# Opening of a layernorm, FFT and Mish kernel: rows centred on ScalarE, roots taken by pairs, w1 scaled in four parts

## The chip, the cores and the metric

One core of a Trainium2 chip runs the whole program. The metric is device time in us, the median of several executions. The engines are TensorE (PE, with its weight loads PEld), VectorE (DVE), ScalarE (ACT), GpSimd (POOL) and SyncE (SP, which here only issues DMAs). Each runs its own list of instructions in order and waits on semaphores of the others.

## The reference

x is 2048 rows of 512; w1 is 512 x 1792, w2 is 1792 x 512. All of it is float32.

```python
xn = (x - mean(x)) / sqrt(var(x) + 1e-5)               # by row
A  = irfft2(rfft2(xn) * (w_r + 1j * w_i), s=(2048, 512))
h  = einsum("bsd,df->bsf", xn, w1) + b1
B  = einsum("bsf,fd->bsd", h * tanh(softplus(h)), w2)  # Mish between
return x + A + B
```

## The kernel before

**Numbers.** A float32 operand is split into two float16 parts, a high half (scaled and rounded, on ScalarE) and a low half (the rest, on VectorE), and a product is three matmuls: high by high, high by low, low by high. The scales are powers of two, got from a norm of the data.

**Work.** The 2048 rows are taken in 4 groups `g` of 4 tiles `s` of 128 rows. Normalized rows `xh` feed two branches. In the MLP branch, `up(n)` makes one tile `ph` of 128 hidden units by 512 rows (12 matmuls of 512 columns, from `w1t` and the transposed rows `xnT`), `mish(n)` is ScalarE's function from `ph` to `hb`, `a_hi(n)` and `a_lo(n)` split the result, and `down(n)` adds it into `pa` with w2 (12 matmuls). There are 56 `up` and 56 `down`. In the spectral branch, `s1_mm` is the first stage of the transform along the rows (bank psS, emptied by `s1_out`, stored by `s1_store`), and later stages are `p2_unit`, `spectrum` (banks `dre`, `dim`; result split into `u`), `dp_unit` (bank psA, emptied into `at`, sent by DMA into `ai`), `ip_unit` (psT, `tt`) and `s1_inverse` (psY).

**Order.** `opening()` and `middle()` are written out by hand, and each engine does their steps in the written order. From there a scheduler interleaves the streams by priority. PSUM banks come from three pools: `ps_f` (2), `ps_h` (2), `ps_a` (4); a new tile waits until the old one in its bank is emptied. `big` has 5 SBUF buffers for the chunks of w1, then of w2.

**The opening.** `warm` makes 24 matmuls on a tile of zeros, which no result uses. x's first group comes in two DMAs of 512 KB, then part of the constants and w1 in 7 chunks. VectorE computes mean and variance of four tiles (`stats`, `aggr`); `root_by_table` takes the root of all four variances (ScalarE's Sqrt), loads ScalarE's table for Mish, and makes `rs` (the inverse deviation times 1024) and `nb` (minus mean times `rs`). By tile, ScalarE's `hi` makes the high half from x, `rs` and `nb`; VectorE's `full` makes the float32 row `xs` and `lo` subtracts the high half. TensorE turns the halves (`turn_to`, 4 matmuls with the identity, into `pt`), and `place_from` copies them into `xnT`. w1's chunks are scaled in three parts (chunk 0, chunk 1, chunks 2 to 6): `norm_w1` takes the squares' sum on ScalarE (or a bound from the maximum on VectorE), `sum_w1` is GpSimd's sum over the partitions, `scale_w1` makes the scale `ip_w`, `w1_hi` and `w1_lo` split, `exp_w1` makes the scale that `mish` undoes. `act_scale` makes the scale `ip_a` of `a` from all parts. `up_pair(0)` and `up_pair(2)` make the first four `ph`, all high by high first; `up(4)` and on go one by one.

Functions that the diff touches, and their callers, with the line numbers of the profile:

Of the kernel before, what the change touches and what calls it, by code (L numbers as in the profile page):

```python
# [19 lines left out]
P = 128  # L20
# [16 lines left out]
def spectral_mlp_kernel(ctx, tc, x, wt, w0, w1, b1, w2, cT, cIT, cM, out):  # L37
# [71 lines left out]
    class Rows:  # L109

        def __init__(self, g, x4):
# [6 lines left out]
            self.xh, self.xs, self.pt = {}, {}, {}  # L118
# [7 lines left out]
        def root_by_table(self):  # L126
            var = self.mv[:, :, 1]
            eps = sp.tile([P, 1], F32, tag="eps", name="eps")
            nc.gpsimd.memset(eps, 1e-5)
            d, v, y, t, z, k = (  # L130
                sp.tile([P, 4], F32, tag=f"{tag}4", name=f"{tag}_0", bufs=2)
                for tag in ("rd", "rv", "ry", "rt", "rz", "rk")
            )
# [126 lines left out]
    def norm_w1(k, engine):  # L260
        part = min(k, 2)
# [27 lines left out]
    def w1_hi(k):  # L289
        fs = slice(2 * k * P, 2 * (k + 1) * P)  # L290
        nc.scalar.activation(w1t[:, 0, :, fs], w1st[k], AF.Copy, scale=sc["w1", min(k, 2)])

    def w1_lo(k):
# [4 lines left out]
            sc["w1", min(k, 2)],  # L298
# [562 lines left out]
    def opening():  # L861
# [16 lines left out]
        for s in range(4):  # L878
            r.stats(s)
            if s:  # L880
                r.aggr(s - 1)
# [452 lines left out]
```

## Time and profile before

| | |
|---|---|
| median of 3 runs | 373.16 us (372.67 to 373.53) |
| profiled execution, its own time | 373.16 us |
| its span, from the first to the last instruction | 371.4 us |
| TensorE busy | 364.4 us (98%) |
| VectorE busy | 250.0 us (67%) |
| ScalarE busy | 170.6 us (46%) |
| granted TensorE clock | 1.000 |

The execution's time is 1.76 us more than its span. Times in rows count from the span's start. Busy time of TensorE includes the 24 products on zeros, and its matmuls are pipelined: a record lasts longer than the distance to the next one.

### The profile page before, as it was taken

How to read it: one execution, taken by the hardware profiler on the slowest of the kernel's cores; microseconds unless marked ns; L12 is line 12 of the kernel's file. 1: busy time of each engine (PE TensorE's matmuls, PEld its weight loads, DVE VectorE, ACT ScalarE, POOL GpSimd, SP SyncE). 2: the span in 40 equal slices, each digit the busy share in tenths (PEclk: the TensorE clock that was granted, in tenths of full speed). 3: DMA queues.
4: the chain of work that ended last, by engine and by line, in shares of the span. 5: the costliest groups of instructions: out<-in, count | busy, mean ns of one | idle time of the engine just before them, and what ended most of it. 6: DMA issues, size and time to landing. Idle time of an engine off the chain costs nothing.

```text
span 371.4 us, 5651 instructions
## 1 busy us (share of the span) xinstructions
PE 364.4 (98%) x2093; PEld 186.0 (50%) x2093; DVE 250.0 (67%) x471; ACT 170.6 (46%) x257; POOL 46.7 (13%) x48
## 2 busy tenths in 40 slices
PE   8899999999999999999999999999999999999996
PEld 3544444544544455444555455544545444445564
DVE  4878998654467754599888866878479854424354
ACT  3889986424533533433544353445435444523100
POOL 0110003302203300203030303030030300000000
PEclk9999999999999999999999999999999999999999
DMA  8844921697673588036302360105931234549535
GB/s 280 262 135 158 327 62 28 175 336 235 192 181 124 103 220 277 8 115 238 102 3 71 103 187 39 43 23 164 282 115 46 65 90 98 128 93 339 222 142 199
DMA packets 56012, 55.79 MB, mean 150 GB/s; under 512 B 16128, under 2 KB 44704, under 8 KB 55216
## 3 DMA queue, kind: packets, MB, share of 16 engines
q1 hardware_dynamic: 55984, 55.43, 48.7%
q8 instruction: 16, 0.26, 0.3%
q14 instruction: 12, 0.10, 0.1%
HBM read 35.46 MB, written 12.58 MB: 129 GB/s over the span
## 4 chain that ended last, share of the span: by engine, by line
PE 90%; DVE 3%; DMA 3%; ACT 1%; SPq 1%; issue 1%; ACTq 0%; DVEq 0%
PE ph L642 38%; PE pa L65 12%; PE pa L64 12%; PE pa L61 12%; PE psP L454 1%; PE psY L61 1%; DMA x<-in_x_dram 1%; PE psY L65 1%; PE psP L464 1%; PE psY L64 1%; PE psT L61 1%; PE psS L64 1%; PE psS L61 1%; PE psT L65 1%; PE psS L65 1%; PE psT L64 1%
## 5 line engine op out<-in xcount | busy, mean ns | idle before, releaser
L642 PE MATMUL ph<-xnT,w1t 128*128 128x512 f16 x672 | 153.7, 379 | 0.0
L642 PEld LDWEIGHTS <-w1t 128*128 128x128 f16 x672 | 65.1, 98 | 74.0 <-issue 0.2
L653 ACT ACTIVATE hb<-ph,b1t,fp_exp 128x512 f32<-128x512 f32 x56 | 43.2, 773 | 77.4 <-PE ph L642 77.3
L65 PE MATMUL pa<-w2t,a 128*128 128x512 f16 x181 | 68.6, 379 | 0.0
L61 PE MATMUL pa<-w2t,a 128*128 128x512 f16 x181 | 68.6, 379 | 0.0
L64 PE MATMUL pa<-w2t,a 128*128 128x512 f16 x181 | 68.6, 379 | 0.0
L665 DVE SCALAR_TENSOR_TENSOR a<-hb,ip_a,a 128x512 f16<-128x512 f32 x46 | 35.9, 783 | 37.4 <-ACT a L662 37.2
L662 ACT ACTIVATE a<-hb,ip_a 128x512 f16<-128x512 f32 x46 | 32.9, 719 | 1.0
L65 PEld LDWEIGHTS <-a 128*128 128x128 f16 x190 | 18.6, 98 | 21.0
L61 PEld LDWEIGHTS <-a 128*128 128x128 f16 x190 | 18.6, 98 | 19.2
L64 PEld LDWEIGHTS <-a 128*128 128x128 f16 x190 | 18.6, 98 | 18.9
L194 POOL TENSOR_TENSOR xh<-xs,xh 128x512 f16<-128x512 f32 x12 | 15.7, 1308 | 62.8 <-ACT xh L178 32.9
L610 DVE SCALAR_TENSOR_TENSOR tt<-psT,tt 128x512 f16<-128x512 f32 x16 | 11.0, 686 | 17.3 <-ACT tt L609 17.3
L469 DVE SCALAR_TENSOR_TENSOR z<-psP,z 128x512 f16<-128x512 f32 x16 | 10.9, 690 | 13.6 <-ACT z L468 13.6
L178 ACT ACTIVATE xh<-x,nb,rs 128x512 f16<-128x512 f32 x16 | 12.7, 803 | 13.0 <-DVE nb L169 12.9
L363 ACT ACTIVATE u<-w,sc_u 128x512 f16<-128x512 f32 x16 | 10.8, 713 | 15.4 <-DVE w L563 7.0
L609 ACT ACTIVATE tt<-psT 128x512 f16<-128x512 f32 x16 | 9.5, 592 | 17.6 <-PE psT L65 13.9
L586 ACT ACTIVATE at<-psA 128x512 f16<-128x512 f32 x16 | 9.4, 586 | 13.3 <-PE psA L65 10.3
L468 ACT ACTIVATE z<-psP 128x512 f16<-128x512 f32 x16 | 9.5, 594 | 12.3 <-PE psP L464 12.3
L364 DVE SCALAR_TENSOR_TENSOR u<-w,sc_u,u 128x512 f16<-128x512 f32 x16 | 11.5, 748 | 5.4 <-ACT u L363 5.4
L97 ACT ACTIVATE y<-psS 128x512 f16<-128x512 f32 x16 | 9.3, 589 | 12.0 <-PE psS L65 12.0
L98 DVE SCALAR_TENSOR_TENSOR y<-psS,y 128x512 f16<-128x512 f32 x16 | 10.9, 686 | 5.8 <-ACT y L97 5.8
(204 smaller groups left out, 566.4 us busy)
## 6 DMA issues: line engine op xcount, KB each, us to landing
wm<-in_wt_dram SPq DMA_DIRECT2D x8, 512.0 KB
ai<-at SPq DMA_DIRECT2D x64, 64.0 KB
d_t<-tt SPq DMA_DIRECT2D x32, 128.0 KB
w1s<-in_w_dram SPq DMA_DIRECT2D x7, 512.0 KB
w2s<-in_w_dram SPq DMA_DIRECT2D x7, 512.0 KB
d_y<-y SPq DMA_DIRECT2D x7, 512.0 KB
m<-in_x_dram SPq DMA_DIRECT2D x3, 1024.0 KB
yt<-d_y SPq DMA_DIRECT2D x6, 512.0 KB
```

The costliest lines, as they stand in the source:

```text
L61: first = nc.tensor.matmul(ps, stat(0), mov(0), start=start, stop=False)
L64: nc.tensor.matmul(ps, stat(0), mov(1), start=False, stop=False)
L65: nc.tensor.matmul(ps, stat(1), mov(0), start=False, stop=stop)
L98: nc.vector.scalar_tensor_tensor(y1v[:, :, 1, :], psv, 2.0**-17, y1v[:, :, 0, :], op0=ALU.mult, op1=ALU.subtract)
L178: nc.scalar.activation(xh[:, 0, :], self.x[s], AF.Identity, scale=self.rs[:, s : s + 1], bias=self.nb[:, s : s + 1])
L194: engine.tensor_sub(self.xh[s][:, 1, :], self.xs[s], self.xh[s][:, 0, :])
L364: nc.vector.scalar_tensor_tensor(dst_l, src, scale, dst_h, op0=ALU.mult, op1=ALU.subtract)
L610: nc.vector.scalar_tensor_tensor(tt[:, :, 1, :], ps, 2.0**-12, tt[:, :, 0, :], op0=ALU.mult, op1=ALU.subtract)
L642: nc.tensor.matmul(ph[n + k], w1t[:, hw, dc, f * P : (f + 1) * P], xnT[g][:, hx, dc, :], start=(hw, hx, dc) == (0, 0, 0), stop=(hw, hx, dc ...
L653: nc.scalar.activation(hbt[n], ph.pop(n), AF.Mish, bias=b1t[:, f : f + 1], scale=s_exp[part_of(f)])
L662: nc.scalar.activation(act[n][:, 0, :], hbt[n], AF.Copy, scale=sc["a"])
L665: nc.vector.scalar_tensor_tensor(act[n][:, 1, :], hbt.pop(n), sc["a"], act[n][:, 0, :], op0=ALU.mult, op1=ALU.subtract)
```

## The change

Row 0 of x has a DMA of its own. Each tile is centred on ScalarE as soon as its mean is there (`xc` = mean minus x), and the roots are taken for two tiles at a time. The sign goes into `nk` (minus 1024 by the approximate inverse root) and `rs`, which one Newton step refines from it. The high half is `xc` by `nk`, on ScalarE. The low half is `xc` by `rs` less the high half, one VectorE instruction instead of two. The high half no longer waits for the Newton step. The table for Mish is loaded later, after w1's second square. Warming is 13 products, and 3 more stand between the first turns. Two tiles are placed by one copy. w1's chunks 2 to 6 become two parts (2 and 3; 4 to 6), and the first chunk's high half is made in two pieces. `s1_out` of tiles 0 and 1 goes from the opening into `middle`. In `dp_unit`, the two instructions that empty psA have high priority.

```diff
-        def root_by_table(self):
-            var = self.mv[:, :, 1]
...
-            nc.scalar.activation(d, var, AF.Sqrt, bias=eps)
-            nc.scalar.preload_act_table_set("mish")
-            nc.vector.tensor_scalar(v, var, 1e-5, -0.5, op0=ALU.add, op1=ALU.mult)
...
+        def root_by_table(self, lo, hi):
...
+            nc.scalar.activation(d, var, AF.Sqrt, bias=self.eps)
+            yield
             nc.vector.reciprocal(y, d)
...
+            nc.vector.tensor_scalar(k, y, -1024.0, None, op0=ALU.mult)
+            yield
+            nc.vector.scalar_tensor_tensor(t, y, -0.5, y, op0=ALU.mult, op1=ALU.mult)
+            nc.vector.scalar_tensor_tensor(z, var, 1e-5, t, op0=ALU.add, op1=ALU.mult)
+            nc.vector.scalar_tensor_tensor(rs, z, 1.5, k, op0=ALU.add, op1=ALU.mult)
+            yield
+
+        def centre(self, s):
+            nc.scalar.activation(self.xc[s], self.x[s], AF.Identity, scale=-1.0, bias=self.mv[:, s, 0:1])
+
+        def hi_centred(self, s):
+            self.xh[s] = tp.tile([P, 2, D], F16, tag=f"w{s}", name=f"xh_{s}")
+            nc.scalar.activation(self.xh[s][:, 0, :], self.xc[s], AF.Copy, scale=self.nk[:, s : s + 1])
+
+        def lo_centred(self, s):
+            xh = self.xh[s]
+            nc.vector.scalar_tensor_tensor(
+                xh[:, 1, :], self.xc[s], self.rs[:, s : s + 1], xh[:, 0, :], op0=ALU.mult, op1=ALU.subtract
+            )
...
-    W1_PARTS = [(0, 1), (1, 2), (2, 7)]
+    W1_PARTS = [(0, 1), (1, 2), (2, 4), (4, 7)]
...
+            with tc.high_priority():
+                nc.scalar.mul(at[:, :, 0, :], ps, 2.0**-15)
+                nc.vector.scalar_tensor_tensor(
+                    at[:, :, 1, :], ps, 2.0**-15, at[:, :, 0, :], op0=ALU.mult, op1=ALU.subtract
+                )
...
-        warm(24)
+        idle = warm()
+        idle(13)
         x0 = tp.tile([P, 4, D], F32, tag="z", name="x_0")
-        for a in (0, 2):
-            nc.sync.dma_start(x0[:, a : a + 2, :], xv[:, a : a + 2, :])
+        for a, b in ((0, 1), (1, 2), (2, 4)):
+            nc.sync.dma_start(x0[:, a:b, :], xv[:, a:b, :])
...
+        turn(0, 0)
+        turn(1, 0)
+        idle(3)
+        place(0, 0, DVE)
+        r.lo_centred(3)
+        scale_w1(0)
...
+        place(0, 1, ACT)
+        place(1, 0, DVE)
+        w1_hi(0, 0, 1)
+        w1_hi(0, 1, 2)
+        place(1, 1, DVE)
         norm_w1(1, ACT)
         sum_w1(1)
-        norm_w1(2, ACT)
+        nc.scalar.preload_act_table_set("mish")
         w1_lo(0)
         scale_w1(1)
         exp_w1(0)
         w1_hi(1)
-        norm_w1(3, ACT)
+        norm_w1(3, DVE)
+        norm_w1(2, ACT)
+        sum_w1(2)
         up_pair(0, (0, 1), (1, 0))
+        mish(0)
+        w1_lo(1)
         norm_w1(5, DVE)
         norm_w1(4, ACT)
-        norm_w1(6, DVE)
-        sum_w1(2)
-        mish(0)
-        bias_max()
+        scale_w1(2)
         exp_w1(1)
-        act_min()
-        w1_lo(1)
-        mish(1)
-        scale_w1(2)
-        up_pair(2, (0, 1), (1, 0))
-        act_scale()
         exp_w1(2)
         w1_hi(2)
+        norm_w1(6, DVE)
+        sum_w1(3)
+        mish(1)
+        up_pair(2, (0, 1), (1, 0))
         w1_lo(2)
+        bias_max()
+        act_min()
+        w1_hi(3)
+        scale_w1(3)
+        act_scale()
...
-        s1_out(0, ps1[0])
-        s1_out(1, ps1[1])
-        s1_store(1)
...
         row_in(r, 0)
+        s1_out(0, ps1[0])
         w2_part(2)
         down(1)
         row_in(r, 1)
+        s1_out(1, ps1[1])
+        s1_store(1)
```

ScalarE's list before, from the root (`rd`) to the high half of w1's first chunk (`xh_s` high halves of the rows, `w1t,qw1` a square of a chunk, `xnT<-pt` a placing):

```order
L134 ACTIVATE rd_0_154<-mv_0_140,eps_152 128x4
L135 ACT_TABLE_LOAD
L178 ACTIVATE xh_0_169<-x_0_121,nb_0_142,rs_0_141 128x512
L178 ACTIVATE xh_1_174<-x_0_121,nb_0_142,rs_0_141 128x512
L267 ACTIVATE w1t_89,qw1_0_179<-w1s_0_125 128x4x256
L178 ACTIVATE xh_2_183<-x_0_121,nb_0_142,rs_0_141 128x512
L178 ACTIVATE xh_3_191<-x_0_121,nb_0_142,rs_0_141 128x512
L207 COPY xnT_0_143<-pt_0_00_196 128x4x128 x2
L291 ACTIVATE w1t_89<-w1s_0_125,ip_w1_0_188 128x4x256
```

and of the change, to the first chunk's two pieces (`xc_0` holds rows 0 and 1, `xc_1` rows 2 and 3):

```order
L145 ACTIVATE xc_0_137<-x_0_110,mv_0_130 128x512
L134 ACTIVATE rd_0_148<-mv_0_130,eps_135 128x2
L145 ACTIVATE xc_0_137<-x_0_110,mv_0_130 128x512
L149 ACTIVATE xh_0_156<-xc_0_137,nk_134 128x512
L149 ACTIVATE xh_1_158<-xc_0_137,nk_134 128x512
L145 ACTIVATE xc_1_138<-x_0_110,mv_0_130 128x512
L134 ACTIVATE rd_2_168<-mv_0_130,eps_135 128x2
L145 ACTIVATE xc_1_138<-x_0_110,mv_0_130 128x512
L149 ACTIVATE xh_2_177<-xc_1_138,nk_134 128x512
L280 ACTIVATE w1t_89,qw1_0_179<-w1s_0_115 128x4x256
L149 ACTIVATE xh_3_183<-xc_1_138,nk_134 128x512
L217 COPY xnT_0_133<-pt_0_01_140 128x2x4x128
```

Four centrings (L145) come in between, the root stands twice, the table load has left this stretch, and one placing of 1024 elements stands where two of 512 did.

VectorE's list before, from the last statistics to the low half of row 0:

```order
L124 BN_AGGR mv_0_140<-st_0_139 128x2 x2
L136 TENSOR_SCALAR rv_0_155<-mv_0_140 128x4
L137 RECIPROCAL ry_0_156<-rd_0_154 128x4
L138 TENSOR_TENSOR rt_0_157<-ry_0_156 128x4
L139 TENSOR_SCALAR rk_0_159<-ry_0_156 128x4
L140 TENSOR_TENSOR rz_0_158<-rt_0_157,rv_0_155 128x4
L141 SCALAR_TENSOR_TENSOR rs_0_141<-rz_0_158,rk_0_159 128x4
L142 SCALAR_TENSOR_TENSOR nb_0_142<-mv_0_140,rs_0_141 128x4
L184 TENSOR_SCALAR xs_0_171<-x_0_121,mv_0_140,rs_0_141 128x512
L194 TENSOR_TENSOR xh_0_169<-xs_0_171,xh_0_169 128x512
```

and of the change, from the statistics of row 1 on:

```order
L121 BN_STATS st_0_129<-x_0_110 128x6
L124 BN_AGGR mv_0_130<-st_0_129 128x2
L136 RECIPROCAL ry_0_149<-rd_0_148 128x2
L137 TENSOR_SCALAR nk_134<-ry_0_149 128x2
L121 BN_STATS st_0_129<-x_0_110 128x6
L124 BN_AGGR mv_0_130<-st_0_129 128x2
L139 SCALAR_TENSOR_TENSOR rt_0_150<-ry_0_149 128x2
L140 SCALAR_TENSOR_TENSOR rz_0_151<-mv_0_130,rt_0_150 128x2
L141 SCALAR_TENSOR_TENSOR rs_0_131<-rz_0_151,nk_134 128x2
L121 BN_STATS st_0_129<-x_0_110 128x6
L124 BN_AGGR mv_0_130<-st_0_129 128x2
L153 SCALAR_TENSOR_TENSOR xh_0_156<-xc_0_137,rs_0_131,xh_0_156 128x512
```

The reciprocal and `nk` of the first two rows stand ahead of the statistics of row 2, and each low half (L153) is one instruction.

ScalarE's list before, in the scheduled part, around the second half of the spectrum of the last column block (`at_11<-psA_11` empties a bank, `u_3` is the split of the first half, `es1_3<-dim1_3` reads the next `dim`):

```order
L586 ACTIVATE at_10_2987<-psA_10_2974 128x4x128
L653 ACTIVATE hb_3_4_3016<-ph_3_4_3003,b1t_91,fp_exp_2_370 128x512
L662 ACTIVATE a_3_4_3018<-hb_3_4_3016,ip_a_367 128x512
L363 ACTIVATE u_3_2825<-w1_0_3_2894,sc_u_1444 128x512
L363 ACTIVATE u_3_2825<-w3_0_3_2896,sc_u_1444 128x512
L586 ACTIVATE at_11_3034<-psA_11_3021 128x4x128
L491 COPY es1_3_3066<-dim1_3_3062 128x512
```

and of the change:

```order
L603 ACTIVATE at_10_2994<-psA_10_2981 128x4x128
L670 ACTIVATE hb_3_4_3023<-ph_3_4_3010,b1t_91,fp_exp_2_321 128x512
L679 ACTIVATE a_3_4_3025<-hb_3_4_3023,ip_a_377 128x512
L603 ACTIVATE at_11_3041<-psA_11_3028 128x4x128
L379 ACTIVATE u_3_2832<-w1_0_3_2901,sc_u_1451 128x512
L379 ACTIVATE u_3_2832<-w3_0_3_2903,sc_u_1451 128x512
L507 COPY es1_3_3073<-dim1_3_3069 128x512
```

`at_11` moved ahead of the two splits of `u_3`. VectorE's list has the same move.

## Rows read from the trace of the kernel before

**Rows 1.** Page, part 1: busy us (share), number of instructions.
```profile
PE 364.4 (98%) x2093; PEld 186.0 (50%) x2093; DVE 250.0 (67%) x471; ACT 170.6 (46%) x257; POOL 46.7 (13%) x48
```

**Rows 2.** Chain of waits in order of time: start us, us, what.
```profile
0.72 3.66 DMA x<-in_x_dram
...
7.70 1.28 ACT L135
...
13.85 0.70 DVE xh L194
14.60 0.40 PE pt L202 x4
16.31 36.31 PE ph L642 x168
```

**Rows 3.** Who TensorE waited for: us in total, times, longest.
```profile
PE pt L202 <- ACT xh L178: 1.4, 4, 0.5
...
PE dim L61 <- DVE at L587: 0.2, 1, 0.2
```

**Rows 4.** Timeline of ScalarE: start, us, what, count [idle before].
```profile
7.39 0.30 ACT L134 ACTIVATE rd<-mv,eps 128x4 f32<-128x4 f32 x1 [5.39 <-DVE mv L124]
...
9.00 1.52 ACT L178 ACTIVATE xh<-x,nb,rs 128x512 f16<-128x512 f32 x2
10.42 1.04 ACT L267 ACTIVATE w1t<-w1s 128x1024 f16<-128x1024 f32 x1
...
12.87 1.04 ACT L207 COPY xnT<-pt 128x512 f16<-128x512 f16 x2
...
25.66 0.71 ACT L662 ACTIVATE a<-hb,ip_a 128x512 f16<-128x512 f32 x1
```

**Rows 5.** Timeline of VectorE.
```profile
4.41 1.29 DVE L121 BATCH_NORM_STATS2 st<-x 128x6 f32<-128x512 f32 x2 [4.41 <-DMA x<-in_x_dram]
...
8.52 0.16 DVE L142 SCALAR_TENSOR_TENSOR nb<-mv,rs 128x4 f32<-128x4 f32 x1
...
12.96 0.15 DVE L230 TENSOR_SCALAR ip_w<-qs 128x1 int32<-128x1 int32 x1
13.14 0.15 DVE L233 TENSOR_SCALAR ip_w<-ip_w 128x1 int32<-128x1 int32 x1
...
14.46 2.07 DVE L207 COPY xnT<-pt 128x512 f16<-128x512 f16 x6
16.45 1.27 DVE L295 SCALAR_TENSOR_TENSOR w1t<-w1s,ip_w,w1t 128x1024 f16<-128x1024 f32 x1
...
26.40 0.75 DVE L665 SCALAR_TENSOR_TENSOR a<-hb,ip_a,a 128x512 f16<-128x512 f32 x1 [0.58 <-ACT a L662]
```

**Rows 6.** Timeline of TensorE (PE) and of its weight loads (PEld), opening.
```profile
1.30 8.27 PE L859 MATMUL ps_w<-z_w 128*128 128x512 f16 x24 [1.30 <-POOL eps L129]
...
10.57 0.62 PE L202 MATMUL pt<-cTt,xh 128*128 128x128 f16 x8 [0.31 <-ACT xh L178]
...
16.15 14.19 PE L642 MATMUL ph<-xnT,w1t 128*128 128x512 f16 x65
...
6.82 0.15 PEld L859 LDWEIGHTS <-z_w 128*128 128x128 f16 x1 [0.28 <-issue]
7.25 1.83 PEld L859 LDWEIGHTS <-z_w 128*128 128x128 f16 x9 [0.28 <-issue]
```

**Rows 7.** Timeline of GpSimd.
```profile
11.70 0.59 POOL L277 PARTITION_ALL_REDUCE qs<-qw  x1 [10.41 <-ACT w1t L267]
```

**Rows 8.** Windows: engines busy, PEclk, DMA share, GB/s, fourth us.
```profile
3.00:4.00 1.00, 1.00 (x4) 0.44 (x3) 0.00 (x0) 0.00 (x0) 0.00 (x0) 1.00 1.02 397
```

**Rows 9.** Timeline of the up-products: VectorE, ScalarE, and weight loads.
```profile
24.54 1.28 DVE L295 SCALAR_TENSOR_TENSOR w1t<-w1s,ip_w,w1t 128x1024 f16<-128x1024 f32 x1 [0.30 <-ACT w1t L291]
...
43.87 0.77 ACT L653 ACTIVATE hb<-ph,b1t,fp_exp 128x512 f32<-128x512 f32 x1
...
44.69 7.43 PEld L642 LDWEIGHTS <-w1t 128*128 128x128 f16 x35 [0.17 <-issue]
```

More of the change, by code (lines that the diff above doesn't have):

```diff
@@ L248, in spectral_mlp_kernel, with w1_part @@
     sc = {}
-    W1_PARTS = [(0, 1), (1, 2), (2, 7)]
+    W1_PARTS = [(0, 1), (1, 2), (2, 4), (4, 7)]
     w1st, w1q = {}, {}
+    def w1_part(k):
+        return next(i for i, (a, b) in enumerate(W1_PARTS) if a <= k < b)
     def part_of(f):
-        return min(f // 2, 2)
+        return w1_part(f // 2)
     def load_w1(c, t):
@@ L260, in norm_w1 @@
     def norm_w1(k, engine):
-        part = min(k, 2)
+        part = w1_part(k)
         a, b = W1_PARTS[part]
@@ L857, in warm, with idle @@
         ps = ps_f.tile([P, D], F32, tag="f", name="ps_w")
-        for _ in range(n):
-            nc.tensor.matmul(ps, z[:, :P], z, start=True, stop=True)
+        def idle(n):
+            for _ in range(n):
+                nc.tensor.matmul(ps, z[:, :P], z, start=True, stop=True)
+        return idle
     def opening():
-        warm(24)
+        idle = warm()
+        idle(13)
         x0 = tp.tile([P, 4, D], F32, tag="z", name="x_0")
-        for a in (0, 2):
-            nc.sync.dma_start(x0[:, a : a + 2, :], xv[:, a : a + 2, :])
+        for a, b in ((0, 1), (1, 2), (2, 4)):
+            nc.sync.dma_start(x0[:, a:b, :], xv[:, a:b, :])
         load_ct(0)
@@ L877, in opening @@
         r = Rows(0, [x0[:, s, :] for s in range(4)])
[L878 to L881, printed above, removed]
-        r.aggr(3)
-        r.root_by_table()
-        for s in range(4):
-            r.hi(s)
-            r.full(s)
-            r.lo(s, DVE)
-            if s == 1:
-                norm_w1(0, ACT)
-                sum_w1(0)
-            if s == 2:
-                scale_w1(0)
+        r.nk = sp.tile([P, 4], F32, tag="nk", name="nk")
+        r.eps = sp.tile([P, 1], F32, tag="eps", name="eps")
+        nc.gpsimd.memset(r.eps, 1e-5)
+        xc = [tp.tile([P, 2, D], F32, tag="X", name=f"xc_{k}", bufs=2) for k in range(2)]
+        r.xc = [xc[s // 2][:, s % 2, :] for s in range(4)]
         pts = {}
@@ L897, in opening, with turn, place @@
                 pts[k, h] = pool.tile([P, 2, 4, P], F16, tag=tag, name=f"pt_0_{k}{h}")
-        def pt_of(s, h):
-            return pts[s // 2, h][:, s % 2]
+        def turn(s, h):
+            r.turn_to(pts[s // 2, h][:, s % 2], s, h)
+        def place(k, h, engine):
+            r.place_from(pts[k, h], k, h, engine)
+        r.stats(0)
+        r.aggr(0)
+        r.centre(0)
+        r.stats(1)
+        r.aggr(1)
+        root = r.root_by_table(0, 2)
+        next(root)
+        r.centre(1)
@@ new lines, in opening @@
+        next(root)
+        r.hi_centred(0)
+        r.hi_centred(1)
+        r.stats(2)
+        r.aggr(2)
+        r.centre(2)
+        next(root)
+        r.stats(3)
+        r.aggr(3)
+        root = r.root_by_table(2, 4)
+        next(root)
+        r.centre(3)
+        r.lo_centred(0)
+        next(root)
+        r.hi_centred(2)
+        norm_w1(0, ACT)
+        sum_w1(0)
+        r.hi_centred(3)
+        r.lo_centred(1)
+        next(root)
+        r.lo_centred(2)
+        turn(0, 0)
+        turn(1, 0)
@@ L914, in opening @@
[L914 to L926 removed]
+        turn(2, 1)
@@ L1015, in opening @@
         mish(9)
+        s1_out(3, ps1[3])
+        s1_store(3)
         a_hi(9)
@@ L1049, in opening @@
         a_lo(13)
-        return r
+        return r, ps1
     def row_in(r, s):
@@ L1076, in w2_part, with middle @@
         w2_lo(c)
-    def middle(r):
+    def middle(r, ps1):
         load_ct(2)
@@ L1184, in spectral_mlp_kernel @@
     with tc.manual_schedule():
-        r1 = opening()
-        n_up, n_down = middle(r1)
+        n_up, n_down = middle(*opening())
     done[0] = n_up + n_down
```

92 lines of the change are left out of this document (35 added, 57 removed).

## The prediction

> **What bounds the kernel now.** I read the page first: TensorE is busy 364.4 of 371.4 us [rows 1], so the first question is where it is not busy with useful work. The chain of waits, in order of time, answers it. It runs through the load of x (0.72 to 4.38), VectorE's statistics, ScalarE's table load at 7.70, the last half-row on VectorE (13.85), four turns on TensorE (14.60), and then stays on TensorE's up-products for 36.31 us in one piece [rows 2]. So two regimes: up to 16.15, where the first up-product starts [rows 6], the end is set by a serial chain over DMA, VectorE and ScalarE; behind it TensorE is full, and one us won ahead of 16.15 is one us of the kernel, as long as nobody lets TensorE wait later. TensorE's own list of waits confirms it: 1.4 us in the opening for ScalarE's rows, and among the few later ones 0.2 us of `dim` for an emptying of psA [rows 3]. The warming products hide the rest of the opening's idleness: 24 of them fill 1.30 to 9.57 and compute nothing [rows 6].
>
> The profiled execution took 373.16 us, the median of the three runs, so a difference made on its trace can be taken off the median directly.
>
> **The opening, costed.** An engine starts its next instruction about 0.1 us before the record of the last one ends (two rows on ScalarE take 1.52 us, so a step there is 0.71), so I step with duration less 0.1, and take some 0.2 per link where a small VectorE instruction needs the one before (12.96, 13.14) [rows 4, 5].
>
> *Row 0 alone.* Before, 512 KB land at 4.38. The DMA engines move 397 GB/s in that stretch [rows 8], so the 256 KB that need no longer be waited for are 0.66 us at most, and 0 at the least, if the landing is all latency. I take 0.6: row 0 lands at 3.8, and row 1 at 4.4 as before, since the same bytes stand ahead of it. The third issue pushes the later loads on SP back by one issue; nothing reads w1 before 10, and the DMA engines are busy throughout (share 1.02).
>
> *Statistics and centring.* Statistics take 0.61 a step (1.29 for two) [rows 5]. Row 0 has its mean at 4.65, row 1 at 5.5. ScalarE centres row 0 from 4.75 (priced as the old row instruction, step 0.71; without the second operand it may be 0.61, as the split of `a`, 0.71 long), takes the root of two rows at 5.6 (0.30), centres row 1 to 6.5. VectorE's reciprocal and `nk` are done by 6.3. So the high halves of rows 0 and 1 run at 6.5 and 7.1, against 9.00 and 9.7 before. What went: the wait for all four means, the four dependent instructions between reciprocal and `nb` (to 8.68), and the table load, 1.28 us on the chain [rows 2, 4, 5].
>
> *Rest of ScalarE.* Centre row 2 (7.7), root (8.45), centre row 3 (8.65), high half of row 2 (9.4 to 10.1), square of w1's first chunk (1.04), high half of row 3 (11.05 to 11.75), one placing of 1024 elements (0.9 step, twice the 0.47 of 512), to 12.6. The four centrings are new work, 2.8 us; the two placings of 512 become one of 1024 [rows 4].
>
> *VectorE.* One instruction of 0.75 (priced as the low half of `a`) replaces two per row, of which the second alone is 0.70 [rows 2]. Low halves at 8.3, 9.2, 10.4; placing (0,0) at 11.0 (two steps of 0.33); low half of row 3 waits for ScalarE, 11.8 to 12.5. The all-reduce (0.59) of the square is ready by 11.9, so the two `ip_w` follow at 12.5 and 12.65, and placing (1,0) runs 12.75 to 13.4, (1,1) to 14.0 [rows 4, 5, 7].
>
> *The first up-product* needs half of w1's first chunk: ScalarE from 12.9, 0.71 long, 13.6. TensorE itself has turns (0.055 each at full clock) and S1 products (12 in 1.3 us behind the last turns) and with the last low half at 12.55 it ends them at 13.5 [rows 2, 6]. So up-products start at 13.65 instead of 16.15: **2.5 us**. If row 0 gains nothing and centring costs the full step, I get 14.3 (1.85 us); with the short step 13.35 (2.8 us).
>
> **Does the stream stay fed?** The first two pairs take 10.4 us (48 steps of 0.216), so up(4) starts at 24.0 and needs chunk 2 of w1. Before, its low half ended at 25.82 for a use at 26.5 [rows 9]: 0.7 us of slack, because its scale waited for five chunks. Now the scale waits for chunks 2 and 3 alone. Walking the lists: low half of chunk 0, 1.27 long, to 15.5 [rows 5], squares and maxima of chunks 1 to 3 and chunk 1's split to 18.9, scale of chunks 2 and 3 at 20.8, chunk 2's high half to 21.95 and low half to 23.5. Slack 0.5.
>
> The moved table load (1.28) now stands between the square and the high half of chunk 1: 15.15 to 16.45, high half done at 17.6, needed at 18.8. It is hidden by that 1.2. *A rule speaks against this:* the Trainium skill, "ScalarE: Activation LUTs", section "What ACT_TABLE_LOAD costs", puts a switch at about 2.66 us, load and drain together. The trace shows no such second half: load at 7.70, 1.28 long, next instruction at 9.00 [rows 2, 4]. By the page the sum would lose some 0.15 us to a wait on chunk 1; by the row nothing.
>
> Further on the slack is thin in both kernels: before, mish(9) ends at 44.64 and TensorE's weights pause 0.17 us at 44.69 [rows 9], where up(11) takes that bank. ScalarE's list from the up-products' start to there now has one square less (1.04, chunk 3 on VectorE) and two psS copies less (some 0.5 each, as copies of 512 elements from PSUM), and 1.28 for the table load more: about 0.7 us less work. It loses what it formerly had ready ahead. I book 0.1 for such waits; bounds 0 and 0.6.
>
> The two emptied psS of rows 0 and 1 return behind down(0) and down(1), 0.5 on ScalarE and up to 0.75 on VectorE each. Behind them queue chunks 2 and 3 of w2 and rows 1 and 2. Cover: w2's chunk 2 is first read by down(4), four blocks of 2.6 us later; without it the price would be their 1 to 1.2 us. The store of row 1's result now stands on SP ahead of the first two transposes; those feed up(14), eight downs later. Nothing.
>
> **psA urgent.** In the last quarter, `at_11` goes ahead of two splits of `u` on ScalarE and VectorE, and `dim` waits for that bank: 0.2 us back [rows 3], bounds 0 and 0.4 (the splits come later by as much, but their readers are behind a wait for `dim`'s copy).
>
> Sum: 2.5 + 0.2 − 0.1 = 2.6, so 373.16 − 2.6 = **370.6 us**.
>
> **Rivals.**
> *The clock comes late.* Before, weights of the warming products come every 0.43 us up to 7.25 and every 0.2 from there: the two levels, 1.2 and 2.4 GHz, the rise after 6 us of work without a gap [rows 6]. Now the 13 products end at about 6.85 and the first turn comes at about 7.3 with gaps behind it. If TensorE is at half speed there, its 5.1 us of turns, S1 and three idle products become 10.2. By a rise at time t it has done (t − 7.3)/2 of them, and ends at 8.75 + t/2. With a rise in the middle of the opening, at 10.7, the up-products start at 14.1; with one at 12.5, at 15.0: 0.45 to 1.35 us less gain, time 371.1 to 372.0. For it: fewer products ahead. Against: the old gaps of some 0.3 to 0.5 us did not lower the granted clock. The Trainium skill, "TensorE: Matmul & The Clock Gate", Part 1, says that half rate is the default, that activity releases it, and that the moment differs from run to run; by that rule single runs would scatter between this case and mine, and the one trace here cannot tell.
>
> *Given back in the feed.* If scaling in four parts delays chunk 2, or ScalarE falls behind at mish(7) to mish(10), TensorE stands there; the chunk's slack is 0.5, so a feed 2 us slower than walked returns 1.5 to 2.5 us: 372.1 to 373.2. Against: the part has fewer inputs than before.
>
> *Slower.* The place is the same stretch at half clock right through: with turns and S1 at 10.2 us from 7.3 on, the up-products start at 17.5, 1.35 us later than before, less 0.2 late: 374.3. It decides against the change if the rise comes after 15.2, where 8.75 + t/2 passes 16.35 and the whole gain is spent. Before, a like density of work between 9.9 and 16 held full clock, which speaks against it.
>
> **Chances.** My case 0.66, its own range 370.0 to 371.2 (13.35 to 14.3, feed 0 to 0.6, late 0 to 0.4); late clock 0.16; given back 0.11; slower 0.07. The range from 369.9 to 372.1 takes in my case and the late clock, about 8 in 10. A measurement tells 0.2% (0.75 us) from no change: faster means below 372.4. Of the third rival a quarter is below that: faster 0.84, same 0.09, slower 0.07.
>
> **What would show it.** Right: high half of row 0 near 6.5; first up-product near 13.7; no gap on TensorE over 0.3 us from there to the first down; no wait of `dim` for `at`; the last of the 168 up-products 2.3 to 2.6 us earlier than 52.6 (16.31 + 36.31). Wrong: S1 products at 0.2 us instead of 0.11 (clock), up(4) waiting for w1's low half, a second pause behind the moved table load, or ScalarE still the last to release the up-products well behind 14.3.

## The result, and the profile after

The changed kernel took 373.96 us (median of 20 runs, 372.56 to 376.51) against 373.13 us (20 runs) of the kernel before on the same chip: ratio 1.0031, 95% interval 1.0018 to 1.0044, slower by 0.3%. The forecast was 370.6. The profiled execution took 373.67 us. One run of h3, below, took 644.0 us at a mean granted clock of 0.558, and its ratio leaves that run out.

Page of the changed kernel, busy us and share [answers to rows 1]; then all that TensorE waited for, in us, times, longest [rows 3]:

```profile
PE 362.3 (97%) x2085; PEld 185.9 (50%) x2085; DVE 250.8 (67%) x474; ACT 172.0 (46%) x260; POOL 46.4 (12%) x49
```
```profile
PE pt L212 <- DMA cTt<-in_cT_dram: 2.3, 1, 2.3
PE ps_w L878 <- POOL eps L902: 1.3, 1, 1.3
PE psY L61 <- DMA yi_z<-d_t: 1.2, 1, 1.2
PE ph L659 <- DMA xnT<-xh: 0.6, 1, 0.6
PE psT L61 <- DVE tt L627: 0.2, 1, 0.2
```

Two things came as forecast: the wait of `dim` is gone, and the waits of the turns for ScalarE's rows [rows 3] too. But three waits are for DMA, in the opening, at 77 us and at 334 us, where the forecast had none. The first starts in the loads, as VectorE's timeline shows [rows 5]:

```profile
3.69 0.69 DVE L121 BATCH_NORM_STATS2 st<-x 128x6 f32<-128x512 f32 x1 [3.69 <-DMA x<-in_x_dram]
4.51 0.66 DVE L121 BATCH_NORM_STATS2 st<-x 128x6 f32<-128x512 f32 x1
7.27 0.69 DVE L121 BATCH_NORM_STATS2 st<-x 128x6 f32<-128x512 f32 x1 [1.09 <-DMA x<-in_x_dram]
8.54 0.69 DVE L121 BATCH_NORM_STATS2 st<-x 128x6 f32<-128x512 f32 x1
```

Row 0 is there at 3.67 (3.8 forecast), but rows 2 and 3 only at 7.25; before, they were there at 5.70, and row 2's statistics ran without a wait:

```profile
5.72 0.69 DVE L121 BATCH_NORM_STATS2 st<-x 128x6 f32<-128x512 f32 x1
```

TensorE meanwhile (timeline of the changed kernel, opening) [rows 6]:

```profile
8.18 1.01 PE L212 MATMUL pt<-cTt,xh 128*128 128x128 f16 x8 [2.26 <-DMA cTt<-in_cT_dram]
8.98 1.49 PE L878 MATMUL ps_w<-z_w 128*128 128x512 f16 x3
...
14.88 5.34 PE L659 MATMUL ph<-xnT,w1t 128*128 128x512 f16 x24
```

The turns need the identity, which lies in the constants `cT`; these landed at 8.13, 6.44 before. In that pause, at 8.06, the granted clock fell to half, as the windows show (the column ahead of the DMA share is the clock):

```profile
6.00:8.00 2.00, 0.00 (x0) 0.10 (x1) 0.87 (x3) 1.62 (x3) 0.00 (x0) 1.00 0.89 278
...
9.00:10.00 1.00, 1.00 (x5) 0.28 (x3) 0.96 (x4) 0.53 (x2) 0.00 (x0) 0.50 1.09 376
10.00:11.00 1.00, 1.00 (x8) 0.78 (x7) 0.96 (x5) 0.94 (x2) 0.00 (x0) 0.50 1.10 349
...
12.00:13.00 1.00, 1.00 (x16) 0.93 (x14) 1.00 (x3) 1.00 (x4) 0.41 (x1) 1.00 1.11 338
```

Up-products start at 14.88: 1.27 us won where 2.5 were forecast. By the starts of TensorE's products against the kernel before, 0.38 (at `dim`) and 0.29 (at `psT`) are won later, 0.75 is lost near 77 us and 1.03 near 334 us. Another 0.73 is lost behind the last product, which starts at 367.80 (368.01 before) in a span of 371.9 (371.4). The chain of waits names the first two of these three losses (`xnT` by the transposes of group 1; `tt` is stored to `d_t` and read back from there as `yi`) [rows 2]:

```profile
71.31 6.38 DMA xnT<-xh
...
329.16 3.38 DMA d_t<-tt
332.72 2.75 DMA yi_z<-d_t
```

The third is the last store: from issue to landing 1.60 us before, 2.45 now, with fifteen of its sixteen parts there 0.87 us ahead of the last. The DMA view from 368.5 to 371.0, in 40 slices, shows the late part behind a gap, and a load of instructions beside it:

```profile
GB/s 361 328 328 393 181 115 123 238 303 230 148 25 0 8 164 270 287 304 74 8 0 0 0 0 0 8 16 25 16 0 0 0 0 0 0 0 0 0 0 0
...
q14 instruction: 1, 0.01, 1.4%
```

That load is one packet of 8 KB, 0.55 us long to 370.13; the late packets begin as it ends.

### The profile page after: what moved, and what is told of

It is laid out like the page before. It is cut to its first block, busy times and chain, and to the rows that moved or that the text cites. A ratio compares the mean times of both kernels' runs of the same rounds, so it can differ in the third digit from the quotient of the medians.

```text
span 371.9 us, 5641 instructions
## 1 busy us (share of the span) xinstructions
PE 362.3 (97%) x2085; PEld 185.9 (50%) x2085; DVE 250.8 (67%) x474; ACT 172.0 (46%) x260; POOL 46.4 (12%) x49
## 4 chain that ended last, share of the span: by engine, by line
PE 73%; DVE 12%; DMA 5%; ACT 4%; SPq 2%; issue 2%; POOL 0%; ACTq 0%; DVEq 0%
PE ph L659 28%; PE pa L65 10%; PE pa L64 10%; PE pa L61 10%; DMA xnT<-xh 2%; DVE w2t L374 2%; DMA x<-in_x_dram 2%; DVE w1t L310 1%; ACT w1t L304 1%; DVE q L353 1%; PE psP L470 1%; PE psY L61 1%; PE psY L64 1%; PE psP L480 1%; PE psY L65 1%
## 5 line engine op out<-in xcount | busy, mean ns | idle before, releaser
L204 POOL TENSOR_TENSOR xh<-xs,xh 128x512 f16<-128x512 f32 x12 | 14.8, 1232 | 64.7 <-ACT xh L188 33.3
L604 DVE SCALAR_TENSOR_TENSOR at<-psA,at 128x512 f16<-128x512 f32 x16 | 11.0, 688 | 7.3 <-ACT at L603 7.2
L188 ACT ACTIVATE xh<-x,nb,rs 128x512 f16<-128x512 f32 x12 | 9.6, 804 | 12.9 <-DVE nb L182 12.9
```

Source lines behind the costliest of these rows:

```text
L204: engine.tensor_sub(self.xh[s][:, 1, :], self.xs[s], self.xh[s][:, 0, :])
L604: nc.vector.scalar_tensor_tensor(at[:, :, 1, :], ps, 2.0**-15, at[:, :, 0, :], op0=ALU.mult, op1=ALU.subtract)
```

## The experiments

Each is compared with runs of the kernel before on its own chip. From the profile of each: start of the first up-product; issue time of group 1's fourth transpose; from the issue of the last store of `tt` to the first load of `yi` behind it; last store, issue to landing (us).

| kernel | median | ratio (95%) | up | transpose | store to load | last store |
|---|---|---|---|---|---|---|
| before | 373.13 | 1 | 16.15 | 2.80 | 2.56 | 1.60 |
| changed | 373.96 | 1.0031 (1.0018 to 1.0044) | 14.88 | 4.43 | 3.56 | 2.45 |
| e1_warm22 | 372.90 | 0.9994 (0.9982 to 1.0006) | 14.86 | 2.79 | 2.64 | 2.68 |
| e2_two_loads | 373.26 | 1.0001 (0.9990 to 1.0012) | 14.34 | 4.17 | 2.86 | 2.59 |
| e3_s1_old | 375.06 | 1.0052 (1.0033 to 1.0071) | 15.01 | 4.55 | 3.57 | 2.76 |
| e4_psA_only | 372.92 | 1.0002 (0.9992 to 1.0012) | 16.55 | 2.88 | 2.56 | 1.61 |
| f1_x2_late | 372.26 | 0.9972 (0.9961 to 0.9984) | 15.61 | 1.29 | 2.64 | 1.60 |
| f2_dve8 | 372.08 | 0.9964 (0.9951 to 0.9978) | 15.53 | 2.94 | 2.69 | 1.59 |
| e6_warm_ident | 372.17 | 0.9970 (0.9959 to 0.9982) | 14.78 | 2.97 | 2.65 | 2.77 |
| f4_all | 371.05 | 0.9941 (0.9927 to 0.9955) | 14.88 | 1.28 | 2.68 | 1.60 |
| g1_two_all | 370.86 | 0.9942 (0.9930 to 0.9955) | 14.16 | 1.29 | 2.65 | 1.60 |
| g2_two_no_x2 | 370.67 | 0.9943 (0.9930 to 0.9955) | 14.10 | 3.01 | 2.65 | 1.61 |
| g3_row0_rest | 371.12 | 0.9952 (0.9938 to 0.9966) | 14.94 | 1.29 | 2.65 | 1.61 |
| g4_two_warm13 | 371.33 | 0.9957 (0.9944 to 0.9969) | 14.23 | 2.40 | 2.89 | 1.62 |
| h1_before_one_pool | 388.06 | 1.0411 (1.0392 to 1.0430) | 16.18 | 2.94 | 2.60 | 2.44 |
| h2_dve8_only | 373.70 | 1.0028 (1.0013 to 1.0044) | 16.98 | 4.07 | 3.24 | 1.60 |
| h3_warm7 | 373.35 | 1.0003 (0.9991 to 1.0014) | 16.68 | 4.39 | 2.70 | 1.60 |
| i1_two_warm22 | 371.86 | 0.9967 (0.9957 to 0.9976) | 14.31 | 2.75 | 2.55 | 2.69 |
| i2_no_urgent | 371.39 | 0.9958 (0.9944 to 0.9973) | 14.54 | 2.74 | 2.64 | 1.61 |
| j1_nine_small | 371.43 | 0.9956 (0.9942 to 0.9970) | 14.02 | 2.76 | 2.55 | 2.61 |

**The first theories:** the clock (e1), the loads (e2), SP's order (e3), psA's urgency (e4).

```diff
-        idle(13)
+        idle(22)                                              # e1
-        for a, b in ((0, 1), (1, 2), (2, 4)):
+        for a, b in ((0, 2), (2, 4)):                         # e2
```

> 22 warming products instead of 13, so that TensorE works without a gap until the constants land at about 8.1. Clock theory (the 2.3 us without work drop the granted clock to 1.2 GHz, by chance and for a changing time): full clock from the first rise on in nearly every run, turns at 0.055 and S1 products at 0.11 each, first up-product at 14.0 to 14.5 instead of 14.88, runs within 372.3 to 373.3 and the scatter up to 376.5 gone, median about 372.9. Theory that later transfers give the gain back: full clock too, but the wait of the up-products for group 1's transposes near 77 us grows from 0.6 to 1.0 or more, so that the median stays above 372.7, against 371.9 if all of the opening's gain came through. If the clock is not what scatters: runs still spread over 3 us.

The clock stayed up (one run of twelve under 0.998), and no run is above 373.42; but the first up-product moved by 0.02 only. In both profiles it follows the landing of rows 2 and 3 (7.38 here, 7.25 in the changed kernel), by 7.48 and 7.63 us, so the half clock of the changed kernel's profile had cost 0.15 at most there. Both theories missed something: the 0.75 at 77 us went, where one said that it would grow.

> x in two transfers of two rows again, all else as changed. Load theory (the third transfer in front delays what stands behind it): rows 2 and 3 land at about 5.7 instead of 7.25 and the constants at about 6.4 instead of 8.1, the first turn runs at about 7.0 instead of 8.18, the gap on TensorE shrinks from 2.3 to about 1, the first up-product comes at 14.0 to 14.3, median 373.0 to 373.4. Rival (the late landing is chance or comes from the rest of the queue): constants again at 7.5 to 8.5, row 0 0.6 later at 4.4, median 374.0 to 374.5.

Load theory: rows 2 and 3 at 5.76 and constants at 6.48, as before the change. Up-products at 14.34 although row 0 comes 0.8 later. The first turn ran at 7.86, not at 7.0: it now waits 1.4 us for row 0's high half, and no longer for the constants.

> The emptyings of psS of rows 0, 1 and 3 and their two stores stand where they stood before, all else as changed. Theory that SP's order delays group 1's transposes: the wait of 0.6 at 77 us is gone or under 0.1 and the median falls by about 0.6, to 373.3. Rival (the transposes stand where they stood and the up-products merely come earlier): the wait stays at 0.4 or more, and the median within 0.2 of 374.0; or ScalarE, with 1 us more ahead of the last up-products of group 0, makes TensorE wait there, 0.3 to 1 us.

The five calls (the change also moves the emptying of row 3 and its store, behind `mish(9)`) stand at their old places. The rival: the wait for the transposes stays, and TensorE's waits now name ScalarE, 0.6 us in all, which speaks for the moved emptyings; the medians' intervals (1.0033 to 1.0071 here, 1.0018 to 1.0044 for the changed kernel) overlap:

```profile
PE ph L659 <- ACT hb L670: 0.6, 2, 0.4
PE ph L659 <- DMA xnT<-xh: 0.5, 1, 0.5
```

> The kernel before with psA's emptying urgent, nothing else. As forecast: the wait of dim (0.38 by the starts of the matmuls) is gone and 0.2, at most 0.4 us, come back: 372.7 to 372.9. Rival (the urgent emptying holds up the last emptyings of psT or their stores, and with them the last load for the inverse): the wait of psY for the load grows from 0.2 to about 1, and the time is 373.1 to 373.8.

The wait of `dim` went, the one for `yi` stayed at 0.2, the median did not move. So the urgency does not cause the later wait. Its profile has the half clock from 11.25 to 14.67, behind a pause of 1.45 us: the opening of the kernel before falls at times too, and 26 of the 110 runs of it that stand beside these experiments have a mean of 0.995.

**Later transfers and the end.** All four have 22 warming products. f1 puts `x2 = load_rows(2)`, group 2's rows, behind `row_turn(r, 3)` and its statistics one down later. In e6 the rest of the constants is loaded where all of them were (the last dots below). f4 has the edits of f1, f2 and e6 together. f2 and e6:

```diff
+        dm = sp.tile([P, 1], F32, tag="dm", name="dm")        # f2
+        for _ in range(8):
+            nc.vector.memset(dm, 0.0)
...
+            if a == 1:                                        # e6
+                nc.sync.dma_start(ident, cT[:, :P])
...
```

> The changed kernel with 22 warming products, and the load of group 2's rows (1 MB) issued behind the fourth turn of group 1 instead of ahead of the third; its statistics one down later. Theory that this load holds up the last transposes: the fourth transpose's issue, 2.8 us in the kernel before and 4.4 in the changed one, falls to about 1.4, the wait of the up-products near 77 us is gone in every run, and the runs at 372.8 to 373.4 of the version with 22 products move to 372.0, median 372.0 to 372.4. Rival (the wait was chance of one execution, or VectorE now waits for the rows and holds up w2's last chunk): median 372.7 to 373.3, and for the second part VectorE idle for the load of x near 80 us.

Faster by 0.0022 than e1, but not shown to be for its reason: moving the statistics also took one instruction that only waits off VectorE, and the last store is on time in it. g1 and g2 below settle it.

> The changed kernel with 22 warming products, and eight memsets of one element a partition on VectorE ahead of x's statistics, where it is idle. Theory that the end of the program loses 0.7 to 1.1 us because an 8 KB load of instructions shares a DMA engine with the last store, at a moment that the count of VectorE's instructions sets: the load comes 2 us or more earlier or is not there near the end, the last store lands 1.6 us after its issue instead of 2.4 to 2.7, the span behind the last matmul is 3.3 us instead of 4.1 to 4.4, and all runs are 0.9 us faster than with 22 products alone: 371.0 to 372.5, median 372.0. Rival (the late part is chance, or another engine's stream sets the moment): tail 4.1 to 4.4 as before, median 372.7 to 373.1.

The last 8 KB load of instructions came at 365.0, ahead of the last store's issue at 368.2 (in e1 at 367.7, 1.1 us behind the issue); the store is on time, and the median fell by 0.0030. The theory holds.

> The changed kernel with 22 warming products, and the first 128 columns of the constants (32 KB, the identity) loaded ahead of rows 2 and 3. Theory that the turns' wait for the constants sets the opening: the first turn comes right behind the last warming product at 8.1 or as soon as row 1 is there, and the first up-product at 14.3 or earlier instead of 14.86, so that the median falls by 0.4 or more. Rival (rows 2 and 3, which land at 7.25, set it through ScalarE, whose last half-row and w1's split come at 12.1 to 14.6 whatever TensorE does): the first up-product stays within 0.15 of 14.86, or comes later by what the extra transfer adds to rows 2 and 3, and the median within 0.2 of 372.9.

The profile says the rival (14.78), the median the theory (0.0024 under e1). Rows 2 and 3 landed at 7.3; f1 and f2, with 22 products and no early identity, had them at 8.1 and up-products at 15.5 to 15.6, but e1, with the same loads as these two, had them at 7.38. So the landing differs from execution to execution; why was not settled, and whether the small load ahead of them steadies this was not tried apart either.

> All three together: identity early, the load of group 2's rows behind the turns, eight memsets, with 22 warming products. If each cause is separate: 0.5 to 0.9 from the transposes, 0.9 from the tail, 0 to 0.5 from the opening, against 372.9: 370.8 to 371.5, faster than the kernel before by 0.3 to 0.5%. If the gains were chance of single executions: 372.5 to 373.

It came out at 0.9941.

**Loads, x2 and clock apart.** g1 has two transfers, 22 products, x2 late, eight memsets. g2 has x2 in its old place, g3 `((0, 1), (1, 4))`, g4 `idle(13)`.

> x in two transfers of two rows as before the change, 22 warming products, the load of group 2's rows behind the fourth turn, eight memsets on VectorE; the rest as changed. Theory that the third transfer costs more than row 0 alone gains (rows 2 and 3 land at 7.3 to 8.1 in all profiles with three transfers, at 5.7 with two): rows 2 and 3 by 5.9, statistics of row 2 without a wait, first up-product at 14.3 against 14.8 to 15.6 with three, median 370.4 to 370.8, under the 371.05 of the version with three transfers and the identity early. Rival (the landing is chance and row 0 alone is worth its 0.7): 371.1 to 371.8.

> The same, with the load of group 2's rows where it was, ahead of the third and fourth turns. It prices that load alone. Theory that it holds up the transposes: 0.4 to 0.9 slower in the median than with the load behind the turns, with the fourth transpose's issue at 2.8 or at 4.2 to 4.5 us and a wait of 0 to 0.8 near 76.5. Rival (that wait is a matter of chance and small in the median): within 0.2 of it.

x2's place is worth nothing (0.9942 and 0.9943). In g2 VectorE's statistics (first block) start 0.6 later than in the changed kernel, and none behind the first waits; TensorE (second) has its first turn right behind the warming products:

```profile
4.25 0.69 DVE L121 BATCH_NORM_STATS2 st<-x 128x6 f32<-128x512 f32 x1 [2.52 <-DMA x<-in_x_dram]
5.08 0.66 DVE L121 BATCH_NORM_STATS2 st<-x 128x6 f32<-128x512 f32 x1
6.65 0.68 DVE L121 BATCH_NORM_STATS2 st<-x 128x6 f32<-128x512 f32 x1
```
```profile
8.96 0.61 PE L212 MATMUL pt<-cTt,xh 128*128 128x128 f16 x8
...
14.10 6.22 PE L659 MATMUL ph<-xnT,w1t 128*128 128x512 f16 x28
```

> As the first of these, but x as row 0 alone and rows 1 to 3 in one transfer. If it is the number of transfers that spreads the landing: two again, so rows 1 to 3 land by 5.9, row 0 at 3.5, the first up-product at 14.0 to 14.4, median 370.3 to 370.8. If it is a transfer of one row (256 KB in packets of 2 KB) ahead of the others that brings the 16 DMA engines out of step: rows 1 to 3 land at 7 or later, ScalarE waits for row 1's mean, the first up-product at 15.3 or later, median 371.5 or more.

Between the two: rows 1 to 3 landed at 5.86, so a transfer of one row ahead does not spread the parts. Three transfers do: in e1's profile the parts of rows 2 and 3 came from 5.0 to 7.4, in f1's from 5.2 to 8.1, with two transfers all within 0.9 us. But row 1, now in the later transfer, delays everything that needs its mean, 14.94.

> As the first of these with 13 warming products instead of 22: it prices the clock. Theory that the pause behind 13 products lets the clock fall in some runs: mean granted clock below 0.998 in a third or more of the runs, these 0.4 to 2 us above the others, the others at the time of the version with 22, median 0.2 to 0.6 above it. Rival (the pause of 1.6 us with two transfers is short enough): all runs at 0.999 or more and the same median within 0.15.

No run fell (all 0.999 or more), and yet the median is 0.0015 above g1, with intervals that overlap. At this point the clock was no longer the reason for what 22 products bring. The table hints at one: with 13 the transpose and the store of `tt` take longer.

**What was open** after twelve. h1 puts the bias's `tensor_scalar` on `nc.gpsimd`, h2 is the changed kernel with f2's memsets, h3 the same with `idle(7)`.

> The kernel before, with one instruction of one element a partition (the small number added to the bias's maximum) on GpSimd instead of VectorE; nothing else. Theory that VectorE's instruction count sets where the last 8 KB load of instructions falls: with one instruction less, as in the changed kernel, it falls beside the last store, which lands 2.4 to 2.7 us after its issue instead of 1.6; the span behind the last matmul goes from 3.36 to 4.1 to 4.4 and the median rises by 0.7 to 1.1, ratio 1.002 to 1.003. Rival (the count is not what decides, or the late part is nothing that a median shows): ratio within 0.999 to 1.001, tail 3.3 to 3.4.

The time is spoilt by something else, a stall of 12 us (last section) and a half clock up to 43.91 behind it. But the end tells what was asked: one instruction off VectorE, and the last store of the kernel before takes 2.44 instead of 1.60, with a span of 4.1 us behind the last product. All twenty profiles agree, by the number of VectorE's instructions in the trace, those that only wait for a semaphore included. With 578 (changed, e1, e2, e3, e6, h1, i1, j1) the last store takes 2.44 to 2.77 us; with 579 (before, e4), 577 (f1), and 585 or 586 (the nine with memsets) it takes 1.59 to 1.62.

> The changed kernel with the eight memsets on VectorE alone (13 warming products, three transfers of x). If the tail is a cause by itself: 0.8 to 1.1 us under the changed kernel's 373.96, so 372.9 to 373.2, and still a scatter of 3 us from the clock. Rival (it only helped because the clock was mended too): 373.7 to 374.2.

The store is on time, but the median fell by 0.3 us only, as the rival had it. All twelve runs were at 0.991 to 0.995, and the profile has the half clock from 8.06 to 14.88:

```profile
9.05 1.01 PE L212 MATMUL pt<-cTt,xh 128*128 128x128 f16 x8 [3.13 <-DMA cTt<-in_cT_dram]
...
12.84 1.06 PE L212 MATMUL pt<-cTt,xh 128*128 128x128 f16 x8
...
16.98 3.18 PE L659 MATMUL ph<-xnT,w1t 128*128 128x512 f16 x14
```

Eight turns take 1.06 us, 0.61 in g2. Against f2, whose rows 2 and 3 landed as late (8.07 in both), the up-products start 1.45 later: that is what a long fall costs, bar the 0.2 by which its first turn is later.

> The same with 7 warming products instead of 13, so that the pause ahead of the first turn grows from 2.3 to about 4.5 us. Clock theory: mean granted clock at 0.995 or less in nearly all runs, the half clock reaching behind the first up-product in the profile, where products of 512 columns stand at 0.43 instead of 0.216 us, and a median 0.5 to 2 us above that with 13. Rival (the clock costs nothing, as in the one profile): the same median within 0.3.

Not as the clock theory had it: 0.0025 under h2. With 7 products TensorE reached full clock for the first time at 13.87 and kept it; up-products at 16.68. Four of its runs were at 0.991 to 0.995, seven at 0.999 or more.

i1 is e2 with 22 products, i2 is g2 without `tc.high_priority()`.

> The changed kernel with x in two transfers and 22 warming products, without the memsets, so with VectorE's count as in the changed kernel. Theory that the last store is late in every run: 0.8 to 1.1 us above the version with the memsets (ratio 0.9943), so ratio 0.9965 to 0.9972, last store 2.4 to 2.8 us from issue to landing in the profile. Rival (late in the profile alone, or hidden): ratio 0.994 to 0.995.

> Two transfers, 22 warming products, eight memsets, and psA's emptying at its old priority. If the urgency is worth what its wait shows (0.38 us): ratio 0.9950 to 0.9955 against 0.9943, and the wait of dim back in the profile. Rival (nothing in the median, as when it was added alone): ratio 0.9938 to 0.9948.

Against g2 (0.9943) the late store is worth 0.0024, 0.9 us, and the urgency 0.0015, 0.6 us, the latter with intervals that overlap. In the profiles of i2 and g2, 0.39 us is the wait of `dim`, which is back in i2. Another 0.44 is the opening, where rows 0 and 1 landed at 4.65 instead of 4.22, and at `tt` 0.25 goes the other way.

```diff
...
         idle(13)                                              # j1, with e2's two transfers
+        idle(9, 1)                                            # nine products of one column
...
```

> The changed kernel with x in two transfers and 13 warming products, followed by nine more of a single column, which add 18 instructions to TensorE's stream and almost no work. Theory that the instruction load beside the transposes makes the wait: the 16 KB load falls between 66 and 69, the fourth transpose's issue takes 2.7 to 3.0 us, the wait of 0.54 near 76.5 is gone, and the median falls by 0.4 to 0.6 against the same version without them (ratio 1.0001), to 0.9985 to 0.9990. Rival (chance, or the warming time itself is what mends it): issue 4 us or more and a wait of 0.4 to 0.8, ratio 0.9997 to 1.0005.

It was worth more than expected: 0.9956 against 1.0001, 1.7 us. It is not the clock, since e2's runs at 0.999 or more took 372.62 to 373.66, and j1's 371.18 to 372.05. The DMA view from 70 to 75 us of e2 and SP's timeline there, then both of j1:

```profile
q1 hardware_dynamic: 899, 1.22, 107.1%
q8 instruction: 1, 0.02, 1.1%
```
```profile
69.52 5.55 SPq L208 DMA_TRANSPOSE xnT<-xh  x2
```
```profile
q1 hardware_dynamic: 1974, 1.48, 103.2%
```
```profile
70.00 4.11 SPq L208 DMA_TRANSPOSE xnT<-xh  x2
```

In e2 a 16 KB load of instructions falls beside the transposes, in j1 it falls between 66 and 70. The same from 328.5 to 331 us, beside the last store of `tt`, of e2 and of j1:

```profile
q1 hardware_dynamic: 518, 0.25, 51.1%
q8 instruction: 1, 0.02, 2.5%
```
```profile
q1 hardware_dynamic: 464, 0.22, 45.5%
```

TensorE's waits of e2, 0.6 for `tt`, 0.5 for `yi`, 0.4 at the transposes, are 0.2 for `yi` alone in j1. By the starts of its products j1 wins 0.54 at the transposes and 0.37 at `yi`, the two places that the loads have left. The rest of the 1.7 is not shown to come from the move. In the opening 0.32 is won, where rows 0 and 1 landed 0.33 earlier. At `tt` 0.44 is won, but there a load falls beside the transfers of `at` into `ai` in both kernels. It lasts 1.46 us in e2 and 0.88 in j1, as the DMA view from 307.5 to 311 us and SP's timeline show, e2 first:

```profile
q8 instruction: 1, 0.02, 2.6%
306.96 3.77 SPq L610 DMA_DIRECT2D ai<-at  x4
```
```profile
q8 instruction: 1, 0.02, 1.6%
306.07 3.19 SPq L610 DMA_DIRECT2D ai<-at  x4
```

This place has a load in every kernel (h1, which stalled, aside). Where it lasts 1.30 to 1.60 us, TensorE waits 0.48 to 0.79 for `tt`; where it lasts 0.88 to 1.10, 0.18 at most. What makes it longer or shorter is open.

The table's columns for the transpose and for store to load part the same way in all profiles (h1 aside). With 7 or 13 full products and no small ones the loads lie at 70.4 to 73.5 and 328.6 to 332.6, at the start of the transfer or behind it; the transpose takes 4.1 to 4.6 (g4, with x2 late, 2.40 against 1.29), store to load 2.86 to 3.57 (h3 2.70). With more products the loads lie at 66.8 to 69.4 and 325.9 to 328.7, 1.1 us or more ahead of it; the transpose takes 2.7 to 3.0 (x2 late 1.3, but there the third, beside the load, takes 2.4 to 2.9 without a wait of TensorE), store to load 2.55 to 2.69. Why 0.9 us of one load makes an issue 1.6 us longer, no run shows.

## Why the prediction was wrong

**"Row 0 alone".** Row 0 landed as costed. The step that failed is its second half: the third issue was taken to cost "one issue", and rows 2 and 3 and the constants to come as before. Rows 2 and 3 came 1.5 to 2.4 us later in every profile with three transfers. That late landing released ScalarE's centring of row 2, and so the end of the opening. In six of the nine profiles with three transfers (e1, e3, f1, f2, e6, f4) the first up-product follows the landing of rows 2 and 3 by 7.48 to 7.49 us, whenever that is. The three others had the half clock in the opening (changed 7.63, h3 8.80, h2 8.91), as e3 had without a loss. In the seven versions of the changed kernel with two transfers of two rows it follows the landing of rows 0 and 1 by 9.88 to 9.89 us. With these the walk nearly holds: 14.02 to 14.54 against 13.65 forecast, near the 14.3 that it gave for a row 0 that gains nothing. From e1 to i1 the third transfer cost 0.0027, 1.0 us, of which 0.55 shows in the opening of the profiles.

**"The first turn comes at about 7.3".** The turn needs the identity, which no step of the walk asked for; 8.18. Behind the 2.3 us without work the clock fell; 15 of the 20 runs of the changed kernel have a mean of 0.997 or less (median 374.29, the five others 373.56). A late clock was a rival at 0.16, and a full half-clock opening one at 0.07, but both let the clock rise late: here it rose at 4.65 and fell again. With three transfers falls were the rule with 13 products (all of h2's runs), and the price lay between nothing (e3), 0.15 (profile after) and 1.45 us (h2). So this step is wrong, but even the runs that did not fall miss the forecast by 3 us.

**"As long as nobody lets TensorE wait later".** On this condition one us won ahead of 16.15 was to be one us of the kernel. It is where most was lost, and no rival had the mechanism: the change takes eight warming products and one VectorE instruction away (579 to 578 with those that only wait; the page, which leaves them out, has 471 and 474), and so moves the loads of instructions of both engines to places where a transfer is waited for. In the changed kernel's profile 0.75 us is lost at the transposes, 1.03 at the store of `tt` and 0.73 at the last store, and the opening is 1.23 short of its 2.5. Some 0.6 more was won than the sum had. Half of that is the 0.29 at `psT`, by luck, since the load beside `at` lasted 1.10 us instead of 1.30. Together that is 3.1 us, from a span 2.6 shorter to one 0.5 longer. By pairs of medians TensorE's loads cost 1.7 us (e2 to j1, of which 0.9 shows at the two waits of the profiles), VectorE's 0.9 (i1 to g2). With the third transfer's 1.0 these make 3.6 of the 3.4 us between forecast and result, within what the intervals allow; the clock has its share in the versions with three transfers, and the pairs do not part it from TensorE's loads there.

**What held.** The feed: no wait in the up-products that follow, moved table load and four parts included, and the moved emptyings spare ScalarE's waits of e3. Row 0's high half ran at 6.30 (6.5 forecast). The table load took 16.34 to 17.63 and ScalarE's next instruction began at 17.64. By the Trainium skill, "ScalarE: Activation LUTs", "What ACT_TABLE_LOAD costs", as much again should have followed; the trace does not agree. The urgency: `dim` no longer waits, which is worth 0.38 in the profiles and 0 (e4) to 0.6 us (i2) in the medians, not clear of noise. With the three causes removed the rest of the change gives 0.9943 (g2, interval 0.9930 to 0.9955): 2.1 us less than the kernel before, where 2.6 were forecast. It beats both kernels. Its terms agree less than its sum: its profile wins 2.04 in the opening, 0.39 at `dim` and 0.31 at `psT`.

**The range.** Its upper end does not follow from the bounds that the prediction names: an up-product at 14.3, 0.6 lost in the feed and nothing won late make 371.9, not 371.2. The measured time is outside by either.

## What to carry to other kernels

When instructions are added or removed, look where the instruction loads (the rows `instruction` in the DMA view) fall afterwards; beside a transfer that TensorE waits for, one cost 0.4 to 1 us here, and a few tiny instructions ahead of it moved it. Ask of every matrix product what all its operands wait for, the identity too. Before splitting a load to have its first part sooner, read when the last part of what stands behind it lands.

## What the runs showed of the hardware that was not expected

A load of instructions is a packet in the same DMA engines as the data: 16 KB (TensorE's, which j1's nine products moved) or 8 KB took 0.3 to 1.8 us of one engine. A transfer that is spread over sixteen waits for that one: of the changed kernel's last store fifteen parts were there at 1.59 us, the last at 2.45. The Trainium skill, "Runtime: NRT & Kernel Launch", section "Instruction fetch mechanics", calls the cost of crossing such a block mostly hidden; the trace agrees for most of them, but not for those here, which cost 0.85 us (last store), 0.5 to 0.75 (transposes) and 0.4 to 1.0 (store of `tt`).

Three transfers of x bring the sixteen parts out of step: those of rows 2 and 3 land over 1.9 us (f4) to 2.95 us (f1), with two transfers over 0.3 to 0.9. Why is open.

In h1 one instruction on GpSimd between two all-reduces stalled it twice, and with it TensorE for 12 us (timeline of GpSimd; idle time in brackets):

```profile
30.42 0.25 POOL L308 TENSOR_SCALAR mb<-mb 128x1 f32<-128x1 f32 x1 [7.99 <-issue]
36.73 0.38 POOL L309 PARTITION_ALL_REDUCE mba<-mb  x1 [6.06 <-issue]
```

The Trainium skill, "GPSIMD Engine Reference", section "Instruction dispatch", gives some 6 us for the first call of a freshly loaded kernel; the trace agrees in size, nearly for the first (7.99) and better for the second (6.06), and shows a stall at both changes of kind; that it is such a load, no run shows.
